# Scores of a head pair in one tile with one store, in nine rooms; four loads of groups at once; k loaded like q and laid out by GpSimd

## The chip, the cores and the metric

The kernel runs on one core of one Trainium2 chip. The metric is the device time of one execution in microseconds (us). The core has five engines that each work through a queue of their own in order: TensorE (PE: matmuls and transposes into PSUM; PEld is its loading of weights), VectorE (DVE), ScalarE (ACT), GpSimd (POOL) and SyncE (SP). Here SP issues nearly all transfers (DMA). They run on 16 transfer engines. An engine waits for another one, or for a transfer, on semaphores, and what stands behind a waiting instruction in the same queue waits too.

## The reference

Attention over 2 batches (B), 12 heads (H), 448 positions (S) and 64 columns per head (D). The heads are mixed by a 12 by 12 matrix ahead of the softmax and by another one behind it:

```
scores = scale * np.matmul(q, k.transpose(0, 1, 3, 2))
scores = np.einsum('bhij,hg->bgij', scores, w_pre)
scores = scores - np.max(scores, axis=-1, keepdims=True)
attn = np.exp(scores)
attn = attn / (np.sum(attn, axis=-1, keepdims=True) + 1e-09)
attn = np.einsum('bhij,hg->bgij', attn, w_post)
return np.matmul(attn, v).astype(np.float32)
```

Its output, 896 rows of 768, goes through an RMS norm and a gated feed-forward layer (silu, width 1536) and then through a second feed-forward layer (elu, width 2048). Everything is float32, w_gate, w_val, w_out and the weights of the second layer come as float64 and are converted on the chip.

## The kernel before

**Layout.** The sequence of a batch is cut into four chunks of 112 positions (CP = 112, NCH = 4); position p * 4 + c stands on partition p of chunk c. Heads go in six pairs (NP = 6). The scores of a pair are computed per chunk: rows of 112 positions of q against all 448 of k. As the mixing runs over heads, the scores go out to a DRAM tile `s_d[b]` in the order position, head, column and come back as groups: a group is ten positions times twelve heads, 120 partitions by 448 columns. There are 45 groups a batch, 90 in all, and a load brings two (LG = 2, 420 KB) into a tile `sg` of which there are four.

**First stage (lines 743 to 762).** `load_first` issues the loads of k and q of batch 0, pair by pair, on SP, into two rooms of the tile "at". k comes through `pair_of`, in pieces of 64 elements (256 bytes); q in pieces of four positions, 1024 bytes. TensorE needs chunk, head, column order. k lies so by its load; q is brought into it by a copy on VectorE (`q_beside`, line 415). Then `turned` (line 441) transposes the pair's k or q, ScalarE copies the result rounded (line 446), VectorE the rest (line 448: the split), and `scores` (line 459) multiplies: high times high, high times low and low times high, two heads, six matmuls. `busy` (line 425) is filler for TensorE. Two pairs behind the turning, `scores(0, i - 2, 0, True)` does chunk 0. `select`, `repeat`, `copies` and `blocks` make the mixing matrices from w_pre and w_post: small VectorE instructions, one matmul (line 141), two copies of it on VectorE (line 149), four selects on GpSimd (lines 155 and 159), and on VectorE the scales vsc (line 165).

**Emptying the scores (line 470, `scores_out`).** Each head's scores are copied from PSUM by ScalarE (line 478) or VectorE (line 476) into a staging room `st`, 112 by 448, of which there are five (and three of the tile "e32" for some of chunk 1), and stored by a transfer of its own (line 479). A copy that finds no free room waits until a store has landed.

**Main loop (line 829).** After chunk 0, line 765 loads the first two groups, EARLY = 4 pairs of chunk 1 are done, and line 770 loads the next two. Then each step t issues, on all engines, parts of several groups: the split of group t + 3 (lines 527 on ScalarE and 528 on GpSimd; every second group needs none), the mixing matmuls of t + 1 (535, or 538 to 540), the maximum of t (547, VectorE), its exponential (555, ScalarE), the normalised halves eh and el of earlier ones (586, 593, VectorE), the second mixing (614) and its copy (626). Loads of groups are issued seven groups ahead (AHEAD = 7). The remaining pairs of scores, the turning of batch 1 and its scores lie in a list `hq` and are popped at 0.5 to 0.8 a step. Loads of v and the second batch's k and q stand on SP between these.

**After it.** Windows of six or seven groups are multiplied with v, normalised (tiles xt and sq) and written as xh and xl; then the feed-forward layers run, with their weights loaded and converted in the tiles raw, w32 and whl of `wpool`.

## Time and profile before

| | us |
|---|---|
| median of 3 runs | 767.53 |
| lowest and highest | 763.04, 774.26 |
| the profiled execution | 771.17 |
| its span, first to last instruction | 769.5 |

| engine | busy us | share of the span | instructions |
|---|---|---|---|
| TensorE | 749.9 | 97% | 5743 |
| its weight loads | 592.2 | 77% | 5743 |
| VectorE | 552.0 | 72% | 1107 |
| ScalarE | 434.4 | 56% | 904 |
| GpSimd | 96.3 | 13% | 117 |

The attention part takes the first 280 us or so, the feed-forward layers the rest. An engine's busy share is a mean over stages with different limits. Matmuls are pipelined and their ends are modelled, so that a busy TensorE is not TensorE at its peak. In rows in order of time, the first number is the start, the second the duration, and what stands in brackets is how long the engine had stood idle before it and what ended that. "xN" counts instructions merged into one row.

### The profile page before, as it was taken

The page shows a single profiled execution, that of the slowest core. Times are in us where ns is not written, and L with a number is a line of the kernel's source. Part 1 is how long each engine was busy: PE and PEld are TensorE (multiplying, and loading weights), DVE is VectorE, ACT ScalarE, POOL GpSimd, SP SyncE. Part 2 cuts the span into 40 slices and gives each one's busy share as a digit, 9 for nine tenths or more (in the row PEclk, how much of TensorE's full clock was granted, in tenths as well). Part 3 has the DMA queues.
Part 4 walks back from the last instruction along what each step waited for, and adds up shares of the span by engine and source line. Part 5 has one row for each costly group of instructions (what it writes and reads, how often), then busy time and mean ns, then how long its engine had stood idle before and what let it go on. Part 6 is the DMA issues. An engine that isn't in the chain of part 4 may idle for free.

```text
span 769.5 us, 14672 instructions
## 1 busy us (share of the span) xinstructions
PE 749.9 (97%) x5743; PEld 592.2 (77%) x5743; DVE 552.0 (72%) x1107; ACT 434.4 (56%) x904; POOL 96.3 (13%) x117
## 2 busy tenths in 40 slices
PE   8899999999898999999999999999999999999997
PEld 7566887777676865555555599999999999999997
DVE  6476999997898947788787766554888787742741
ACT  5377798889578826665667433231776666311310
POOL 1122443443344400000000000000000000000000
PEclk9899999999899999999999999999999999999999
DMA  8898985877654004343323233322443343542612
GB/s 210 276 304 236 172 214 171 248 192 237 174 164 108 3 2 134 114 123 124 122 87 121 83 112 117 100 84 81 123 124 114 92 123 90 160 121 73 168 37 72
DMA packets 92872, 104.04 MB, mean 135 GB/s; under 512 B 21316, under 2 KB 88708, under 8 KB 92804
## 3 DMA queue, kind: packets, MB, share of 16 engines
q1 hardware_dynamic: 92612, 103.04, 47.3%
q8 instruction: 45, 0.74, 0.4%
q14 instruction: 23, 0.19, 0.1%
q10 hardware_dynamic: 192, 0.08, 0.1%
HBM read 81.08 MB, written 22.02 MB: 134 GB/s over the span
## 4 chain that ended last, share of the span: by engine, by line
PE 76%; DVE 13%; DMA 4%; ACT 4%; issue 2%; POOL 1%; SPq 0%; ACTq 0%; POOLq 0%
PE psa_t L200 13%; PE psa_t L199 13%; PE psa_t L201 12%; PE psa_t L1076 4%; PE psa_t L1078 4%; PE psa_t L1077 4%; PE psf_t L201 3%; PE psf_t L199 3%; PE psf_t L200 3%; DVE el L593 3%; DMA s_d<-st 3%; PE pst_t L614 3%; PE psv_t L650 3%; DVE nmax L547 3%; PE psa_t L459 3%; PE psa_t L535 2%
## 5 line engine op out<-in xcount | busy, mean ns | idle before, releaser
L614 PEld LDWEIGHTS <-eh 120*112 120x112 f16 x720 | 67.3, 132 | 28.0 <-issue 19.4
L254 ACT ACTIVATE whl<-w 128x768 fp32r<-128x768 f32 x44 | 37.3, 847 | 84.9 <-DVE w L248 70.7
L226 ACT ACTIVATE w<-raw 128x768 f32<-128x768 f32 x68 | 61.6, 907 | 25.6 <-DVE whl L306 18.9
L258 DVE TENSOR_TENSOR whl<-w,whl 128x768 fp32r<-128x768 f32 x44 | 42.2, 958 | 44.7 <-ACT whl L254 44.7
L528 POOL TENSOR_TENSOR sl<-sg,sh 120x448 fp32r<-120x448 f32 (+1 forms) x45 | 56.5, 1256 | 124.3 <-ACT sh L527 116.9
L200 PE MATMUL psa_t<-x2l,whl 128*128 128x448 f32 x192 | 70.7, 368 | 0.0
L201 PE MATMUL psa_t<-x2h,whl 128*128 128x448 f32 x192 | 70.1, 365 | 0.0
L199 PE MATMUL psa_t<-x2h,whl 128*128 128x448 f32 x192 | 70.1, 365 | 0.0
L555 ACT ACTIVATE e<-psa_t,nmax 120x448 f32<-120x448 f32 (+1 forms) x90 | 57.3, 636 | 22.3 <-DVE rs L570 20.2
L614 PE MATMUL pst_t<-m2h,eh 120*112 120x120 f16 x360 | 63.3, 218 | 2.9 <-ACT at L626 2.8
L614 PE MATMUL pst_t<-m2h,el 120*112 120x120 f16 x360 | 63.2, 219 | 2.9 <-DVE el L593 2.1
L248 DVE SCALAR_TENSOR_TENSOR w<-w,raw 128x768 int32<-128x768 int32 x68 | 65.2, 958 | 1.1
L593 DVE SCALAR_TENSOR_TENSOR el<-e,rs,eh 120x448 f16<-120x448 f32 (+1 forms) x90 | 65.4, 727 | 0.2 <-ACT eh L584 0.2
L242 DVE SCALAR_TENSOR_TENSOR raw<-raw 128x768 int32<-128x768 int32 x68 | 65.0, 956 | 0.0
L614 PE MATMUL pst_t<-m2l,eh 120*112 120x120 f16 x360 | 63.3, 218 | 0.0
L298 ACT ACTIVATE w<-w,gs 128x128 f32<-128x128 f32 x144 | 44.6, 392 | 23.2 <-DVE gs L287 23.2
L650 PE MATMUL psv_t<-at,vs 112*64 112x70 f32 (+3 forms) x1344 | 56.3, 232 | 0.0
L547 DVE TENSOR_REDUCE nmax<-psa_t 120x1 f32<-120x448 f32 (+1 forms) x90 | 54.9, 610 | 0.6 <-PE psa_t L535 0.6
L199 PE MATMUL psa_t<-xhl,whl 128*128 128x448 f16 x150 | 52.9, 353 | 1.0 <-ACT xhl L702 1.0
L626 ACT ACTIVATE at<-pst_t 112x480 f32<-112x480 f32 (+1 forms) x90 | 52.1, 579 | 2.5 <-PE pst_t L614 2.3
L650 PEld LDWEIGHTS psv_t<-at,vs 112*64 112x64 f32 x1344 | 47.1, 140 | 8.3 <-issue 5.1
L1076 PE MATMUL psa_t<-whl,gh 128*128 128x384 f32 x160 | 53.4, 334 | 0.0
(146 smaller groups left out, 1905.6 us busy)
## 6 DMA issues: line engine op xcount, KB each, us to landing
raw<-in_moe_w_out_dram SPq DMA_DIRECT2D x28, 768.0 KB, 4.5
sg<-s_d SPq DMA_DIRECT2D x44, 420.0 KB, 5.1
s_d<-st SPq DMA_DIRECT2D x93, 196.0 KB, 3.5
raw<-in_moe_w_in_dram SPq DMA_DIRECT2D x16, 768.0 KB, 4.6
raw<-in_moe_w_gate_dram SPq DMA_DIRECT2D x12, 768.0 KB, 4.3
raw<-in_moe_w_val_dram SPq DMA_DIRECT2D x12, 768.0 KB, 4.5
vs<-in_v_dram SPq DMA_DIRECT2D x12, 224.0 KB, 6.1
qk<-in_k_dram SPq DMA_DIRECT2D x6, 224.0 KB, 5.1
```

Source lines behind the costliest of these rows:

```text
L199: nc.tensor.matmul(out=ps, lhsT=wh(kk), rhs=xh_(kk), start=(first and kk == 0), stop=False)
L200: nc.tensor.matmul(out=ps, lhsT=wh(kk), rhs=xl_(kk), start=False, stop=False)
L201: nc.tensor.matmul(out=ps, lhsT=wl(kk), rhs=xh_(kk), start=False, stop=(last and kk == nk - 1))
L226: nc.scalar.activation(out=w, in_=raw.bitcast(F32)[:, :, 1], func=ACTF.Abs if small else ACTF.Copy, scale=REBASE)
L242: nc.vector.scalar_tensor_tensor(out=lo, in0=hi, scalar=SIGN, in1=lo, op0=ALU.bitwise_and, op1=ALU.bitwise_or)
L248: nc.vector.scalar_tensor_tensor(out=wi, in0=wi, scalar=3, in1=lo, op0=ALU.logical_shift_left, op1=ALU.bitwise_or)
L547: nc.vector.tensor_reduce(out=nmax[:r], in_=ps[:r, :S], axis=AXX, op=ALU.max, negate=True)
L555: nc.scalar.activation(out=e32[:r], in_=ps[:r, :S], func=ACTF.Exp, bias=nmax[:r], scale=1.0, accum_out=sm[:r])
L593: nc.vector.scalar_tensor_tensor(out=el[:r], in0=e32[:r], scalar=rs[:r], in1=eh[:r], op0=ALU.mult, op1=ALU.subtract)
L614: nc.tensor.matmul(out=o, lhsT=lhs[:r, c * CP:(c + 1) * CP], rhs=rhs[:r, :, :ni], start=(n == 0), stop=(n == 2),)
L650: nc.tensor.matmul(out=psx[s * D:(s + 1) * D, kk, :n], lhsT=vs[b, kk][:, s, c, :], rhs=at[:, c, hh, :n], start=(c == 0), stop=(c == NCH - 1),)
L1076: nc.tensor.matmul(out=o, lhsT=gh[:, kk, tk], rhs=wh[:, j], start=first, stop=False)
```

## The change

Four things are changed, and small ones go with them.

- **Pair tiles.** The two heads of a pair go into one staging tile, 112 by 2 by 448, and one transfer stores both (line 484 of the changed kernel) once the second copy is done. For batch 0 there are nine such rooms: four of the tile whl, two of raw (both for weights, later) and three of st; for batch 1 the three of st.
- **Four loads.** The first four loads of groups (eight groups) are issued one behind the other after chunk 0; the main loop goes on from the fifth. EARLY is 6: all of chunk 1 is done ahead of the main loop.
- **k like q.** k of batch 0 is loaded in 1024-byte pieces as q is, and brought into order by a copy on GpSimd (q's stays on VectorE).
- **Order of the first stage.** The first pair's copies stand first; the small instructions for the mixing matrices follow, `repeat` behind the first pair's transposes, `copies` and `blocks` behind the first splits. k and q of a pair are turned one behind the other, then come the scores. vsc is computed in `post`. xt has two rooms instead of three.

```diff
         def post():
...
             nc.vector.tensor_tensor(out=m2l, in0=m2p, in1=m2h, op=ALU.subtract)
+            for s in range(2):
+                nc.vector.tensor_scalar_mul(
+                    vsc[s * D:(s + 1) * D], cmax.rearrange("p (k s) -> p s k", s=2)[s * D:(s + 1) * D, s], BACK
+                )
...
-                    if tag == "kt":
-                        t = t.rearrange("p (c h d) -> p c h d", h=2, c=NCH)
-                        nc.sync.dma_start(out=t, in_=pair_of(src, 0, p))
-                    else:
...
+                    t = t.rearrange("p (h c d) -> p h c d", h=2, c=NCH)
+                    nc.sync.dma_start(
+                        out=t, in_=src[0, 2 * p:2 * p + 2].rearrange("h (p c) d -> p h c d", c=NCH)
+                    )
...
-        def q_beside(p):
...
+        def beside(p):
+
+            for tag, eng in (("kt", nc.gpsimd), ("qt", nc.vector)):
+                t = ap.tile([CP, NCH, 2, D], F32, tag=tag, name=tag, bufs=2)
+                eng.tensor_copy(out=t, in_=qk_sb[0, p, tag].rearrange("p h c d -> p c h d"))
+                qk_sb[0, p, tag] = t
...
+            st, left = [], [2]
             for s in range(2):
                 dve = s == 1 and (p % 2 == 1 if first else filling[0])
                 late = on_dve if dve else on_act
-                late.append(lambda s=s, dve=dve: scores_out(b, 2 * p + s, c, pss[s], dve))
...
+                late.append(lambda s=s, dve=dve: scores_out(b, p, s, c, pss[s], st, left, dve))
+
+        HOMES = ("whl",) * 4 + ("raw",) * 2 + ("st",) * 3
+
+        def room_of(b, n):
+
+            home = HOMES[n % len(HOMES)] if b == 0 else "st"
+            if home == "st":
+                return ap.tile([CP, 2, S], F32, tag="st", name="st", bufs=3)
+            t = wpool.tile([P, 2 * KD * P], F32, tag=home, name="st_" + home[0], bufs=HOMES.count(home))
+            return t[:CP, :2 * S].rearrange("p (h j) -> p h j", h=2)
+
+        def scores_out(b, p, s, c, ps, st, left, dve):
+            if not st:
+                st.append(room_of(b, c * NP + p))
+            if dve:
+                nc.vector.tensor_copy(out=st[0][:, s], in_=ps[:CP, :S])
             else:
...
+                nc.scalar.activation(out=st[0][:, s], in_=ps[:CP, :S], func=ACTF.Copy)
+            left[0] -= 1
+            if not left[0]:
+                nc.sync.dma_start(out=s_d[b][c * CP:(c + 1) * CP, 2 * p:2 * p + 2, :], in_=st[0])
+                scored[b] = min((c + 1) * CP, S) if p == NP - 1 else c * CP
...
-            xt = ap.tile([P, KD, WMAX], F32, tag="xt", name="xt", bufs=3)
+            xt = ap.tile([P, KD, WMAX], F32, tag="xt", name="xt", bufs=2)
...
-        EARLY, FIRST, FAST, RATE, LATE, AHEAD = 4, 0.5, 0.8, 0.75, 0.6, 7
+        EARLY, FIRST, FAST, RATE, LATE, AHEAD = 6, 0.5, 0.8, 0.75, 0.6, 7
...
         busy(16)
+        beside(0)
         select()
-        repeat()
-        copies()
-        q_beside(0)
-        blocks()
         for i in range(NP + 2):
             if i < NP:
                 turned(*pairs[i], "kt")
                 busy(2)
+                turned(*pairs[i], "qt")
+                busy(2)
+            if i == 0:
+                repeat()
             if i > 1:
                 scores(0, i - 2, 0, True)
-            if i < NP:
-                turned(*pairs[i], "qt")
-                busy(2)
             if i + 1 < NP:
-                q_beside(i + 1)
+                beside(i + 1)
             follow()
+            if i == 0:
+                copies()
+                blocks()
         pre()
         hq = [f for c in range(1, NCH) for f in rows(0, c)]
-        load_group(0, 0)
+        AT_ONCE = 4
+        for g in range(0, AT_ONCE * LG, LG):
+            load_group(0, g)
         for f in hq[:EARLY]:
             f()
             follow()
         hq = hq[EARLY:]
-        load_group(0, LG)
         post()
...
-            if LG * 2 <= t + AHEAD < n and seq[t + AHEAD][1] % LG == 0:
+            if LG * AT_ONCE <= t + AHEAD < n and seq[t + AHEAD][1] % LG == 0:
```

In the built programs the change shows at three places. The first is SP's queue from the last loads of q and k on (qk are their rooms, s_d_88 the scores of batch 0 in DRAM, sg the groups, vs v). Before:

```order
L407 DMA qk_106<-in_q_dram 112x2x256
L479 DMA s_d_88<-st 112x448 x12
L499 DMA sg<-s_d_88 120x2x448
L479 DMA s_d_88<-st 112x448
L479 DMA s_d_88<-st_e 112x448
L479 DMA s_d_88<-st 112x448
L479 DMA s_d_88<-st_e 112x448
L479 DMA s_d_88<-st 112x448
L479 DMA s_d_88<-st_e 112x448
L479 DMA s_d_88<-st 112x448 x2
L499 DMA sg<-s_d_88 120x2x448
L479 DMA s_d_88<-st 112x448 x2
```

The same place in the changed kernel (st_w and st_r are the rooms in whl and raw):

```order
L402 DMA qk_106<-in_q_dram 112x2x256
L484 DMA s_d_88<-st_w 112x896 x4
L484 DMA s_d_88<-st_r 112x896 x2
L504 DMA sg<-s_d_88 120x2x448 x4
L484 DMA s_d_88<-st 112x896 x3
L484 DMA s_d_88<-st_w 112x896 x4
L484 DMA s_d_88<-st_r 112x896 x2
L504 DMA sg<-s_d_88 120x2x448
L376 DMA vs<-in_v_dram 112x2x256
```

Four loads of groups now stand ahead of all stores of chunk 1, where one did, and the next load stands behind nine pair stores.

The second place is the start of VectorE's queue, from its first copies on (setup holds the small tiles of the mixing matrices, par the splits). Before:

```order
L132 COPY setup<-ident 12x120
L133 TENSOR_REDUCE setup<-setup 128x12
L137 TENSOR_SCALAR setup<-setup 128x12
L145 RECIPROCAL setup<-setup 128x12
L149 COPY setup<-psa_t 120x120 x2
L415 COPY qt<-qk_105 112x512
L165 TENSOR_SCALAR vsc<-setup 64x6 x2
L415 COPY qt<-qk_105 112x512
L448 TENSOR_TENSOR par<-psa_t,par 128x448 x2
```

And in the changed kernel:

```order
L411 COPY qt<-qk_105 112x512
L132 COPY setup<-ident 12x120
L133 TENSOR_REDUCE setup<-setup 128x12
L137 TENSOR_SCALAR setup<-setup 128x12
L145 RECIPROCAL setup<-setup 128x12
L411 COPY qt<-qk_105 112x512
L444 TENSOR_TENSOR par<-psa_t,par 128x448 x2
L149 COPY setup<-psa_t 120x120 x2
```

The first q's copy has moved to the front, and the two copies of line 149 from ahead of it to behind the second q's copy and the first pair's two splits.

The third place is the start of GpSimd's queue behind the making of the identity. Before:

```order
masks.py:199 AFFINE_SELECT ident<-ident 128x128
L155 AFFINE_SELECT setup<-setup 120x120
L159 AFFINE_SELECT setup<-setup 120x120
L155 AFFINE_SELECT setup<-setup 120x120
L159 AFFINE_SELECT setup<-setup 120x120
L528 TENSOR_TENSOR sl<-sg,sh 120x448 x10
```

And in the changed kernel:

```order
masks.py:199 AFFINE_SELECT ident<-ident 128x128
L411 COPY kt<-qk_105 112x512 x2
L155 AFFINE_SELECT setup<-setup 120x120
L159 AFFINE_SELECT setup<-setup 120x120
L155 AFFINE_SELECT setup<-setup 120x120
L159 AFFINE_SELECT setup<-setup 120x120
L411 COPY kt<-qk_105 112x512
L411 COPY kt<-qk_106 112x512 x3
L533 TENSOR_TENSOR sl<-sg,sh 120x448 x10
```

The six copies of k are new; the four selects, which wait for the copies of line 149, stand between the second and the third of them.

## Rows read from the trace of the kernel before

**Rows 1.** Stretches: length, busy us (count) by engine, PEclk, DMA share, GB/s.
```profile
6.00:14.00 8.00, 7.34 (x59) 5.63 (x59) 6.37 (x17) 5.05 (x10) 1.41 (x4) 1.00 1.19 246
28.00:32.00 4.00, 1.68 (x7) 0.75 (x5) 0.62 (x1) 1.55 (x3) 1.13 (x1) 0.81 1.06 369
32.00:36.00 4.00, 4.00 (x14) 2.08 (x13) 1.46 (x3) 0.92 (x3) 0.27 (x1) 0.50 0.96 300
36.00:54.00 18.00, 17.79 (x145) 12.62 (x145) 14.38 (x41) 13.39 (x35) 5.84 (x5) 0.96 1.03 319
24.00:68.00 44.00, 38.76 (x301) 26.50 (x301) 27.02 (x77) 26.12 (x63) 9.53 (x8) 0.88 0.95 287
70.00:96.00 26.00, 26.00 (x351) 21.03 (x350) 24.39 (x64) 20.51 (x50) 11.51 (x13) 1.00 0.89 181
320.00:340.00 20.00, 20.00 (x109) 10.39 (x108) 16.20 (x31) 12.34 (x28) 0.00 (x0) 1.00 0.40 119
```

**Rows 2.** Chain of waits, 28 to 72 us: start, us, what (first, last of three).
```profile
25.12 3.91 DMA s_d<-st
...
50.96 7.33 DMA s_d<-st
```

**Rows 3.** Waits by line, 28 to 72 us: us in total, times, longest.
```profile
ACT st L478 <- DMA s_d<-st: 9.1, 5, 4.4
```

**Rows 4.** In order of time, 24 to 71 us: loads, maximum, ScalarE's copies and exponentials.
```profile
24.68 0.38 SPq L499 DMA_DIRECT2D sg<-s_d  x1
...
29.58 0.57 ACT L527 ACTIVATE sh<-sg 120x448 fp32r<-120x448 f32 x1
...
32.78 0.61 DVE L547 TENSOR_REDUCE nmax<-psa_t 120x1 f32<-120x448 f32 x1
...
35.08 0.58 ACT L527 ACTIVATE sh<-sg 120x448 fp32r<-120x448 f32 x1 [3.49 <-DMA sg<-s_d]
...
35.98 0.63 ACT L555 ACTIVATE e<-psa_t,nmax 120x448 f32<-120x448 f32 x1
...
44.85 0.54 ACT L478 ACTIVATE st<-psa_t 112x448 f32<-112x448 f32 x1 [0.81 <-DMA s_d<-st]
...
53.92 0.54 ACT L478 ACTIVATE st<-psa_t 112x448 f32<-112x448 f32 x1 [0.58 <-DMA s_d<-st]
...
58.39 0.54 ACT L478 ACTIVATE st<-psa_t 112x448 f32<-112x448 f32 x1 [2.41 <-DMA s_d<-st]
...
70.10 0.65 ACT L555 ACTIVATE e<-psa_t,nmax 120x448 f32<-120x448 f32 x1
```

**Rows 5.** In order of time, the first stage: TensorE's and VectorE's first pairs.
```profile
6.54 0.40 DVE L149 COPY setup<-psa_t 120x120 f32<-120x120 f32 x2
...
7.53 0.61 PE L441 MATMUL psa_t<-ident,qt 112*128 112x112 f32 x4 [0.66 <-DVE qt L415]
...
8.45 0.43 DVE L415 COPY qt<-qk 112x512 f32<-112x512 f32 x1 [0.46 <-DMA qk<-in_q_dram]
...
8.79 1.15 DVE L448 TENSOR_TENSOR par<-psa_t,par 128x448 fp32r<-128x448 f32 x2
...
9.73 0.57 PE L441 MATMUL psa_t<-ident,qk 112*128 112x112 f32 x4
...
10.46 0.87 PE L459 MATMUL pst_s<-par 64*112 64x448 f32 x6
...
12.62 0.87 PE L459 MATMUL psa_t<-par 64*112 64x448 f32 x6
```

**Rows 6.** By shape: busy us, mean ns, idle before; then two in order of time.
```profile
L155 POOL TENSOR_SCALAR_AFFINE_SELECT setup<-setup 120x120 f32<-120x120 f32 x2 | 0.7, 350 | 5.5 <-DVE setup L149 5.5
...
L586 DVE TENSOR_SCALAR eh<-e,rs 120x448 f16<-120x448 f32 x9 | 4.9, 544 | 0.0
...
47.48 1.36 POOL L528 TENSOR_TENSOR sl<-sg,sh 120x448 fp32r<-120x448 f32 x1 [3.79 <-DMA vs<-in_v_dram]
47.76 1.33 DVE L586 TENSOR_SCALAR eh<-e,rs 120x448 f16<-120x448 f32 x1
```

More of the change, by code (lines that the diff above doesn't have):

```diff
@@ L162, in blocks @@
                 )
-            for s in range(2):
-                nc.vector.tensor_scalar_mul(
-                    vsc[s * D:(s + 1) * D], cmax.rearrange("p (k s) -> p s k", s=2)[s * D:(s + 1) * D, s], BACK
-                )
         def pre():
```

18 lines of the change are left out of this document (removed).

## Prediction

> **What bounds the kernel now.** I read the stretches first, then the chain of waits, then the waits by line, and last the rows in order of time around the places found there. From 320 us on, and in every stretch of the feed-forward part, TensorE is busy without a gap [rows 1]; that part follows the attention part at whatever time attention ends, and no line of it changes. So the change can only move the end of the attention part. Inside it, from 70 to 96 us, VectorE is busy 24.39 of 26 us and TensorE all 26 [rows 1]: the pipeline of 90 groups runs at its engines' pace there, and whatever it starts earlier it ends earlier. What is left to win lies ahead of that.
>
> There the picture differs. From 24 to 68 us the transfer engines are 0.95 busy at 287 GB/s while TensorE works 38.76 of 44 us [rows 1], and the chain of that time holds three stores of scores, the first of 3.91 and the last of 7.33 us [rows 2]: ScalarE wants to empty a PSUM tile into a staging room, all five rooms hold scores whose store has not landed, and, as its queue is in order, everything behind the copy stands too. In all ScalarE waits 9.1 us in this way [rows 3]. The longest of the late ones is 2.41 us, ahead of 58.39 [rows 4].
>
> A second stall is the start. The first load of groups is issued at 24.68; the second stands behind eight stores on SP's queue, so that ScalarE, in order, waits 3.49 us for it until 35.08, and the first exponential, whose maximum VectorE had at 32.78 + 0.61 = 33.39, runs only at 35.98 [rows 4]. From there, step 13 is reached at 70.10: 34.1 us for 13 steps, 2.62 us a step [rows 4].
>
> **The change part by part.** Times are taken against the profiled execution, 771.17 us with a span of 769.5, itself 3.6 above the median of the three runs, 767.53.
>
> *First stage (until the scores of the first 112 rows are stored).* Before, TensorE turned the first q at 7.53 and the third k at 9.73, and from the first scores at 10.46 to the second at 12.62 one pair takes 2.16 us [rows 5]; TensorE has transposes, fillers and scores back to back there, so quicker loads do not shorten the pair. They shorten the way into it. The loads ran at 246 GB/s with every other transfer in 256-byte pieces, where a stretch with long pieces reaches 369 [rows 1]. Two pairs are 0.92 MB, 3.7 us at the one rate, 2.5 at the other: q of the second pair, awaited until 8.45 [rows 5], comes at 8.45 (no gain) to 7.2. I take 7.2, since k then has the pieces that q has. Against it stands the new order: GpSimd's copy of the third k is behind the four selects, these wait for VectorE's two copies of the mixing weights, and these are now behind the second q's copy and the first two splits (they stood ahead of the first q before). 7.2, copy 0.43, splits 1.15, weights' copies 0.40 [rows 5] make 9.2; four selects at 0.35 [rows 6] make 10.6. GpSimd's copy of 512 columns has no row. Below it is VectorE's 0.43 [rows 5], above it GpSimd's own subtraction of 448 columns with two inputs, 1.36 [rows 6], which is 1.55 for 512; one input instead of two speaks for the lower half, and I take 0.9. So the third k is turned at 11.5 instead of 9.73: +1.8. The other copies take 0.9 in each 2.16 and hide behind TensorE; without that cover each would cost the excess over 2.16. A pair's store also leaves when its second half is ready, so the last one has 392 KB instead of 196 ahead of it: +0.6 at 369 GB/s. Together **+2.4** (0 if q comes early enough to free GpSimd in time, +3.7 if it comes at 8.45).
>
> *Four loads at once.* Before, load to first exponential took 35.98 − 24.68 = 11.3. After, the second load is in flight right behind the first and the stores come after both. The first load takes 4.9 at most (24.68 to 29.58 [rows 4], where ScalarE stood in a room wait of 4.4 [rows 3]) and 3.9 at least, what a store half its size takes [rows 2]; I take 4.4. From its copy to the exponential it is 3.8 by the row of the maximum (29.58 to 33.39), 3.5 at the full clock; I take 3.6. 8.0 instead of 11.3: **−3.3** (−2.4 to −3.9).
>
> *Nine rooms for pairs.* After step 0, the waits left of the 9.1 are those of 0.81, 0.58 and 2.41 [rows 4], 3.8 in all. Nine pair rooms hold 3.6 MB, five half-size ones held 1.0, and the nine are used again after about eleven steps. I take the whole: **−3.8** (0 if the wait turns up on the loads instead).
>
> *Clock.* TensorE fell to 0.50 of its clock (the 1.2 GHz level) from about 30 us, after 28 to 32 us in which it worked 1.68 of 4 us; from 32 to 36 it is busy throughout at that level [rows 1], work that takes half as long at the other. After the change it has all six pairs of the second 112 rows, 5.2 us by 0.87 each [rows 5], and the fillers to do meanwhile, against four before. **−1.0** (0 to −2).
>
> *Transfers that come sooner.* What the rooms no longer hold back queues at the transfer engines, and a load of groups issued seven groups ahead stands behind it. **+1.0**, an estimate between 0 and the case below.
>
> *At nothing:* the smaller number of stores (48 for 96) on SP, which is not what anyone waits for there except through the transfers; vsc moved behind the scores, 0.6 us of VectorE while it waits for data; two rooms instead of three for xt, since the order on VectorE has each room's last reader ahead of its next writer; and two pairs of scores that move from the main loop to before it.
>
> Sum: +2.4 − 3.3 − 3.8 − 1.0 + 1.0 = −4.7, that is 766.5 for an execution like the profiled one, and 767.5 − 4.7 = **762.8** as a median.
>
> **Rivals.**
>
> *The transfers bind, the rooms were only where it showed (slower than before).* From 24 to 68 us 44 × 287 = 12.6 MB went through. Two pairs come earlier, 0.8 MB, so 13.4 MB lie ahead of step 13. At 319 GB/s, the rate of 36 to 54 us [rows 1], that is 42.1 us; started at 24.7 + 2.4 = 27.1 it ends at 69.2 instead of 68, at 287 it ends at 73.9: +1.2 to +5.9, I take +3, **770.5**. For it: the share of 0.95 to 1.06. Against it: stores may lag, since their rows are read many steps later, and only loads must be in time. It decides once a load of groups lands later than its copy on ScalarE wants it, four steps after its issue, some 9 us; then ScalarE waits for sg after step 0, which it did not before.
>
> *GpSimd and VectorE stand in each other's way.* A VectorE scaling took 1.33 us at 47.76, where its mean is 0.54, while GpSimd's subtraction ran from 47.48 to 48.84 [rows 6]; it ended 0.25 us after GpSimd. If each q copy so waits out 0.8 us, VectorE needs 0.43 + 1.15 + 0.3 + 0.8 = 2.7 a pair, over TensorE's 2.16, and five pairs cost 2.5 more: −2.2, **765.3**. Against it: k comes first, so that GpSimd is mostly through when q arrives. The Trainium skill, page SBUF — State Buffer, section Who interferes with whom, has it as a rule: VectorE in a two-port mode and GpSimd share a port pair, whoever issues first holds it, and the other blocks fully. The 1.33 us agrees with that.
>
> *The freed steps run faster than I think.* Without the 3.8 us the 13 steps are at 2.33; at 2.1 they save 3.0 more, and if no backlog costs anything the sum is −8.7: **758.8**. For it: from 36 to 54 us VectorE is busy 14.38 of 18 [rows 1]. Against it: a load of groups and the pops fill transfer time in the same steps.
>
> **How the numbers follow.** Forecast 0.52, transfers bind 0.22, ports 0.13, faster steps 0.13. The forecast's terms at their ends give −9.7 and, with the first rival, +5.9, so 757.8 to 773.4; with the scatter of the three runs (763.04 to 774.26) about each case and its weight, 754 to 772 should hold 8 in 10. The likeliest case by itself is 758 to 767. Two per cent is 15 us, about what a measurement of this kernel can tell from no change; none of the cases reaches it, so only scatter does: faster 0.05, within 0.93, slower 0.02.
>
> **What would show it.** First stage right: the first load of groups issued near 27 us and GpSimd's third copy right behind the selects; wrong if it is issued before 25. Loads right: first exponential near 35, no wait of ScalarE for sg ahead of it. Rooms right: ScalarE waits nowhere for a store of scores up to 72 us, and step 13 comes near 65.4. Clock right: no stretch at half clock near 30 us. The forecast is wrong if step 13 comes earlier and the attention part still ends as late, or if ScalarE waits for sg in the steps after the first.

## The result and the profile after

The changed kernel takes 773.31 us (median of 20 runs, 770.85 to 775.16) where the kernel before takes 767.43 us beside it (20 runs, 763.04 to 774.26): the ratio is 1.0068, with a 95% interval of 1.0048 to 1.0088. It is slower by a little over half a per cent, where 762.8 was forecast. The profiled execution took 771.99 us with a span of 769.9.

The stretches of the trace after, in the columns of [rows 1]:

```profile
6.00:14.00 8.00, 4.28 (x27) 3.56 (x26) 4.76 (x12) 2.07 (x4) 3.35 (x7) 0.72 0.95 235
28.00:32.00 4.00, 4.00 (x32) 2.87 (x31) 3.22 (x10) 1.68 (x4) 0.00 (x0) 1.00 0.39 120
32.00:36.00 4.00, 1.85 (x12) 0.88 (x8) 0.62 (x1) 1.01 (x2) 1.07 (x1) 1.00 1.06 249
36.00:54.00 18.00, 17.59 (x119) 11.38 (x120) 12.02 (x33) 10.95 (x27) 4.63 (x5) 0.91 1.03 334
70.00:96.00 26.00, 22.92 (x278) 18.48 (x276) 19.59 (x55) 15.59 (x39) 8.77 (x10) 0.87 1.08 217
```

Two stretches got worse. From 6 to 14 us TensorE works 4.28 of 8 us in place of 7.34, and the granted clock falls to 0.72. From 70 to 96 us it works 22.92 of 26 in place of 26.00, at 0.87. The half clock from 30 us on is not there. But the idle time ahead of it has only moved: from 32 to 36 us TensorE works 1.85 of 4 us, and its clock falls to the half from 36.8 to 40.2.

The places named in the prediction, in order of time (start, us, engine, line, operation; in brackets the idle time before it and what ended it):

```profile
8.27 0.63 POOL L411 COPY kt<-qk 112x512 f32<-112x512 f32 x1 [3.75 <-DMA qk<-in_k_dram]
...
9.13 0.43 DVE L411 COPY qt<-qk 112x512 f32<-112x512 f32 x1 [0.45 <-DMA qk<-in_q_dram]
...
10.88 0.36 POOL L155 TENSOR_SCALAR_AFFINE_SELECT setup<-setup 120x120 f32<-120x120 f32 x1 [1.99 <-DVE setup L149]
...
12.38 1.36 POOL L411 COPY kt<-qk 112x512 f32<-112x512 f32 x2
...
13.05 1.01 PE L437 MATMUL psa_t<-ident,kt 112*128 112x112 f32 x4 [1.92 <-POOL kt L411]
...
15.58 1.17 PE L455 MATMUL pst_s<-par 64*112 64x448 f32 x6
...
16.69 0.61 PE L437 MATMUL psa_t<-ident,kt 112*128 112x112 f32 x4
...
18.05 0.87 PE L455 MATMUL psa_t<-par 64*112 64x448 f32 x6
...
30.08 1.80 SPq L504 DMA_DIRECT2D sg<-s_d  x4
...
34.27 0.58 ACT L532 ACTIVATE sh<-sg 120x448 fp32r<-120x448 f32 x1 [2.87 <-DMA sg<-s_d]
...
36.25 0.58 ACT L532 ACTIVATE sh<-sg 120x448 fp32r<-120x448 f32 x1 [0.97 <-DMA sg<-s_d]
...
39.09 0.63 ACT L560 ACTIVATE e<-psa_t,nmax 120x448 f32<-120x448 f32 x1
...
72.20 0.62 ACT L560 ACTIVATE e<-psa_t,nmax 120x448 f32<-120x448 f32 x1
...
78.14 1.01 PE L437 MATMUL psa_t<-ident,kt 112*128 112x112 f32 x4 [3.08 <-DMA kt<-in_k_dram]
```

Read from the top: GpSimd copies the second k at 8.27, is then given the four selects from 10.88 on, and reaches the third k at 12.38. TensorE, idle meanwhile, turns it at 13.05, where the k of before was turned at 9.73 [rows 5]. The first scores come at 15.58 instead of 10.46 [rows 5], the first load of groups at 30.08 instead of 24.68, the first exponential at 39.09 instead of 35.98, and step 13 at 72.20 instead of 70.10 [rows 4]. At 78.14 TensorE has waited 3.08 us for the k of the second batch.

Waits by line (us in total, times, longest), first from 28 to 72 us and then from 72 to 90:

```profile
ACT sh L532 <- DMA sg<-s_d: 8.9, 5, 2.9
...
PE psa_t L437 <- DMA kt<-in_k_dram: 3.1, 1, 3.1
```

No row of ScalarE waiting for a store of scores is left in 28 to 72 us. The 9.1 us of [rows 3] are gone. Its waits for the groups' scores went from 4.4 us (3.49 and 0.91, both at the start) to 8.9, of which 3.8 stand ahead of the first exponential and 5.0, in three waits, behind it, where before had 0.9 in one. The chain of waits from 6 to 100 us (start, us, what) has the same places:

```profile
2.24 6.87 DMA qk<-in_q_dram
...
12.38 0.62 POOL kt L411
...
25.30 4.57 DMA s_d<-st_r
...
32.93 10.80 DMA s_d<-st
43.75 8.01 DMA vs<-in_v_dram
51.83 9.13 DMA sg<-s_d
...
69.66 8.44 DMA kt<-in_k_dram
```

The chain of 28 to 72 us before held three stores [rows 2]. Now it holds a store, a load of v, a load of groups and a load of k, each of 8 to 11 us.

### The profile page after: what moved, and what is told of

Same layout as the page of the kernel before. It is cut to its first block, busy times and chain, and to the rows that moved or that the text cites. A ratio compares the mean times of both kernels' runs of the same rounds, so it can differ in the third digit from the quotient of the medians.

```text
span 769.9 us, 14571 instructions
## 1 busy us (share of the span) xinstructions
PE 747.3 (97%) x5743; PEld 593.9 (77%) x5743; DVE 548.8 (71%) x1109; ACT 433.5 (56%) x902; POOL 100.0 (13%) x123
## 4 chain that ended last, share of the span: by engine, by line
PE 77%; DVE 10%; DMA 6%; ACT 3%; issue 2%; SPq 1%; POOL 0%; POOLq 0%; ACTq 0%
PE psa_t L200 12%; PE psa_t L198 12%; PE psa_t L199 12%; PE psa_t L1085 4%; PE psa_t L1083 4%; PE psa_t L1084 4%; PE pst_t L619 3%; PE psf_t L198 3%; PE psf_t L200 3%; PE psf_t L199 3%; PE psv_t L655 3%; DVE el L598 2%; PE psa_t L540 2%; DVE nmax L552 2%; PE psa_t L455 2%
## 5 line engine op out<-in xcount | busy, mean ns | idle before, releaser
L241 DVE SCALAR_TENSOR_TENSOR raw<-raw 128x768 int32<-128x768 int32 x68 | 66.6, 979 | 0.0
L1083 PE MATMUL psa_t<-whl,gh 128*128 128x384 f32 x160 | 54.0, 338 | 0.0
L1084 PE MATMUL psa_t<-whl,gh 128*128 128x384 f32 x160 | 54.0, 338 | 0.0
L1085 PE MATMUL psa_t<-whl,gl 128*128 128x384 f32 x160 | 54.0, 338 | 0.0
```

Of the source, the lines that this page charges most:

```text
L241: nc.vector.scalar_tensor_tensor(out=lo, in0=hi, scalar=SIGN, in1=lo, op0=ALU.bitwise_and, op1=ALU.bitwise_or)
L1083: nc.tensor.matmul(out=o, lhsT=gh[:, kk, tk], rhs=wh[:, j], start=first, stop=False)
L1084: nc.tensor.matmul(out=o, lhsT=gh[:, kk, tk], rhs=wl[:, j], start=False, stop=False)
L1085: nc.tensor.matmul(out=o, lhsT=gl[:, kk, tk], rhs=wh[:, j], start=False, stop=end)
```

## The experiments

Each kernel was timed against the kernel before on its own chip, whose median there was 767.2 to 768.9. Two figures go with each: the ratio, and the time at equal clock. Every run lists its granted clock, and over the 111 runs of before that stood beside the experiments the time follows it: a straight line through them gives 499 us per unit of clock, with a standard error of 44 (20 runs under 0.986 have a mean of 771.2 at 0.9840, 16 over 0.995 have 765.4 at 0.9966). Taking 499 × (1 − clock) off each run leaves a time at full clock. It is an estimate by a fit over runs, with an error of about 0.5 us for the mean of a dozen runs. At full clock the kernel before itself stands at 762.5, 763.3, 763.4 and 763.8 on the four chips, so differences of under 1 us between kernels on different chips say nothing.

| kernel | ratio to before, 95% | mean clock | at full clock, us |
|---|---|---|---|
| before | 1 | 0.9903 | 763.2 |
| changed | 1.0068, 1.0048 to 1.0088 | 0.9874 | 766.7 |
| new_start | 1.0051, 1.002 to 1.0082 | 0.9872 | 766.1 |
| old_start | 0.9975, 0.9947 to 1.0004 | 0.9938 | 763.4 |
| old_start_b | 0.9973, 0.9947 to 1.0 | 0.9929 | 763.3 |
| early4 | 1.0087, 1.0052 to 1.0122 | 0.9826 | 765.9 |
| k256 | 1.0, 0.9971 to 1.0029 | 0.9903 | 762.7 |
| sel_late | 0.9999, 0.9978 to 1.0021 | 0.9894 | 763.6 |
| k_vec | 1.0028, 1.0006 to 1.005 | 0.9876 | 764.1 |
| hold | 1.0027, 1.0004 to 1.0049 | 0.9917 | 766.0 |
| rooms | 1.0026, 0.9999 to 1.0053 | 0.9863 | 764.0 |
| loads4 | 1.0062, 1.0032 to 1.0092 | 0.9874 | 767.1 |
| old_qk2 | 0.9998, 0.9974 to 1.0023 | 0.9932 | 764.7 |
| after_qk2 | 1.007, 1.0038 to 1.0102 | 0.9876 | 767.4 |
| old_v1 (5 loads of v left out) | 0.9936, 0.9907 to 0.9965 | 0.9919 | 759.8 |
| old_v1_qk2 (the same) | 0.9926, 0.9897 to 0.9955 | 0.9950 | 760.9 |

### Which half of the change loses the time

The change was cut in two: the first stage (k in long pieces, copies on GpSimd, new order) and the rest (pair tiles, nine rooms, four loads, six pairs ahead).

**old_start**: the changed kernel with the first stage of before.

```diff
-        beside(0)
         select()
+        repeat()
+        copies()
+        q_beside(0)
+        blocks()
         for i in range(NP + 2):
...
+                    if tag == "kt":
+                        t = t.rearrange("p (c h d) -> p c h d", h=2, c=NCH)
+                        nc.sync.dma_start(out=t, in_=pair_of(src, 0, p))
```

> The changed kernel with the first stage of before (k in 256-byte pieces straight into order, no GpSimd copies, the old order of instructions); pair tiles, nine rooms, four loads at once and EARLY 6 stay. Theory START (the new first stage delays the first loads by 5.4 us, from 24.68 to 30.08, and this carries to the end): first loads near 25.3, first exponential near 34, median about 768 (773.3 less 5.4). Theory BATCH 1 (the loss is made at steps 14 to 17, where the turning of the second batch waits for its k and q): the waits of TensorE for kt and qt at 76 to 85 us stay, median 772 to 774.

**new_start**: the kernel before with the new first stage alone.

```diff
+        beside(0)
         select()
-        repeat()
-        copies()
-        q_beside(0)
-        blocks()
         for i in range(NP + 2):
...
-                    if tag == "kt":
-                        t = t.rearrange("p (c h d) -> p c h d", h=2, c=NCH)
-                        nc.sync.dma_start(out=t, in_=pair_of(src, 0, p))
```

> The kernel before with the new first stage alone (k in 1024-byte pieces, GpSimd copies, new order); single rooms and single loads stay. START: first load near 30, everything behind it 5 us later, median about 772.5. BATCH 1: the delay is caught up in the steps that the transfers bind, median 767 to 769.

**early4**: the changed kernel with four pairs of scores ahead of the main loop in place of six.

```diff
-        EARLY, FIRST, FAST, RATE, LATE, AHEAD = 6, 0.5, 0.8, 0.75, 0.6, 7
+        EARLY, FIRST, FAST, RATE, LATE, AHEAD = 4, 0.5, 0.8, 0.75, 0.6, 7
```

> The changed kernel with EARLY back at 4, so that all later pops, and with them the turning of the second batch, come about two pops (2.7 steps) later against the groups. START: no change beyond 1 us, median about 773. BATCH 1: the two waits of 2.6 and 3.2 us at steps 16 and 17 go, median about 768.

Measured: the old first stage under the rest of the change gives 765.97 (0.9975), the new first stage alone gives 772.88 (1.0051). The loss is that of the first stage. Against the profile of before, the exponential of a step starts later (+) or sooner (−) by, in us:

| step | 0 | 4 | 12 | 20 | 36 | 48 | 72 | 89 |
|---|---|---|---|---|---|---|---|---|
| changed | +3.1 | +2.6 | +1.3 | +5.0 | +6.8 | +6.4 | +1.8 | +0.9 |
| new_start | +7.7 | +9.2 | +6.8 | +6.0 | +6.0 | +6.1 | +6.0 | +5.1 |
| old_start | −2.1 | −3.4 | −4.0 | −1.8 | 0.0 | −0.4 | −5.0 | −5.9 |
| early4 | +4.8 | +5.0 | +1.5 | +5.3 | +6.3 | +6.3 | +6.2 | +6.2 |
| rooms | +3.9 | +4.1 | +0.6 | +0.7 | +1.5 | +1.5 | +1.4 | +1.4 |
| loads4 | +9.0 | +8.4 | +8.6 | +7.6 | +9.1 | +8.7 | +4.4 | +3.8 |

new_start has the loop of before, and from step 16 to step 72 it is 6.0 us late without change: what is lost ahead of the loop is not won back. (The two pairs of scores that six pairs ahead take out of the loop stand against the changed kernel, old_start and loads4 up to step 48; at 0.87 us for six matmuls they are 1.7 us of TensorE.) early4 is as late as the changed kernel up to step 48, so the two pairs are not what makes it slow (774.96, where BATCH 1 had 768).

Behind step 48 they help. Between steps 48 and 72 the kernels with six pairs ahead gain 4.2 to 4.7 us on before, in all twelve profiles; the three others with four pairs ahead gain 0.1. Of the gain 1.7 us is the two pairs' work. The rest begins where TensorE waits for VectorE's half el. First before, then the changed kernel:

```profile
197.32 0.26 PE L614 MATMUL pst_t<-m2h,el 120*112 120x120 f16 x1 [2.12 <-DVE el L593]
...
200.00:205.00 5.00, 5.00 (x48) 3.85 (x50) 4.66 (x14) 1.79 (x5) 0.71 (x2) 0.54 0.67 200
```

```profile
200.00:205.00 5.00, 4.03 (x39) 2.90 (x39) 5.00 (x13) 2.77 (x7) 2.38 (x4) 1.00 0.35 96
...
203.04 0.26 PE L619 MATMUL pst_t<-m2h,el 120*112 120x120 f16 x1 [0.97 <-DVE el L598]
```

All four kernels with four pairs ahead run for 6.8 us at half clock somewhere between 197 and 212 us; none of the twelve with six does. In the medians this is not clear of noise: early4's interval (1.0052 to 1.0122) overlaps the changed kernel's.

The profiled executions of before and changed are 771.17 and 771.99: the 0.8 us between them is what step 89 shows. Over all runs the medians are 5.9 apart, since before's profiled execution lay 3.7 above its median and the changed kernel's 1.3 below. old_start's was the fastest of its twelve. So the table shows where time goes, and the runs how much it is.

The first load scatters too: 25.72 to 28.20 us in six profiles with the old first stage and pair tiles (old_qk2, old_start, old_v1_qk2, old_v1, old_start_b, rooms), 30.08, 31.54, 31.63 and 31.95 in four with the new one (changed, after_qk2, early4, new_start). The two groups do not meet.

### What in the first stage

**k256**: the changed kernel, new order kept, k in 256-byte pieces without a copy.

```diff
-        beside(0)
+        q_beside(0)
...
-                beside(i + 1)
+                q_beside(i + 1)
```

> The changed kernel with k loaded as before (256-byte pieces straight into order, no GpSimd copy) in the new order of the first stage. It splits START: if GpSimd's copies and the long pieces cost the 5 us, the first loads are issued near 25.5 and the median is about 768.5; if the order alone (copies of the mixing weights behind the splits, k and q turned one behind the other) costs them, they stay near 30 and the median near 773. BATCH 1: median 772 to 774 either way.

**sel_late**: the changed kernel, the selects and the two copies on VectorE that feed them moved behind the six pairs.

```diff
             follow()
-            if i == 0:
-                copies()
-                blocks()
+        copies()
+        blocks()
         pre()
```

> The changed kernel, with VectorE's two copies of the mixing weights and GpSimd's four selects moved behind the six pairs of the first stage, so that no select stands between GpSimd's copies of k. k keeps its 1024-byte pieces. SELECTS (the first stage loses its time because GpSimd's third copy of k queues behind the selects and TensorE, starved, falls to half clock): the first loads of groups are issued at 26 to 27 us in place of 30.1, no half clock from 9 to 16, and the median is 767 to 769, about that of the version with k in 256-byte pieces (767.6). LANDING (the time goes because the pieces land late and a second engine stands between k and TensorE, the selects only fill a gap that is there anyway): first loads at 29 or later, half clock still there, median 771 or more.

**k_vec**: the changed kernel, k copied by VectorE.

```diff
-            for tag, eng in (("kt", nc.gpsimd), ("qt", nc.vector)):
+            for tag, eng in (("kt", nc.vector), ("qt", nc.vector)):
```

> The changed kernel with the copies of k on VectorE in place of GpSimd; pieces, order and selects as they are. Each pair then has 0.43 more of VectorE's time in place of 0.61 of GpSimd's. SELECTS: no copy of k waits for a select, so first loads at 26 to 27.5 us and a median of 767 to 769. LANDING: TensorE's second and third pair come as late as now (k of the third pair turned near 13), first loads at 29 or later, median 771 or more.

**hold**: the changed kernel with more of TensorE's fillers where it waits.

```diff
                 turned(*pairs[i], "qt")
-                busy(2)
+                busy(14 if i < 2 else 2)
```

> The changed kernel with 12 more of TensorE's fillers behind each of the first two pairs' turned q, where it waits for GpSimd's copies of k. CLOCK (part of the first stage's loss is the half clock of 9.4 to 16.2 us that follows the idle time): no half clock there, the first scores at 14 to 14.8 in place of 15.6, first loads at 28.5 to 29.3 in place of 30.1, median 771.5 to 772.5. QUEUE ALONE (the clock costs nothing of its own, as TensorE waits anyway): first loads stay within 0.5 of 30.1, median 773.

k256 takes 767.63, ratio 1.0: the new order alone does not cost the 5 us; they come with the long pieces and GpSimd's copies. With the selects moved away (sel_late), GpSimd's copies stand one behind the other, and the first scores and loads come sooner. In order of time:

```profile
8.20 0.61 POOL L411 COPY kt<-qk 112x512 f32<-112x512 f32 x1 [3.88 <-DMA qk<-in_k_dram]
...
10.03 0.61 POOL L411 COPY kt<-qk 112x512 f32<-112x512 f32 x1 [1.21 <-DMA qk<-in_k_dram]
...
13.24 1.22 PE L455 MATMUL pst_s<-par 64*112 64x448 f32 x6
...
27.82 1.80 SPq L504 DMA_DIRECT2D sg<-s_d  x4
```

First loads at 27.82 lie between the two bounds given (26 to 27, or 29 and later), but the time is SELECTS': 768.31, ratio 0.9999, within the 767 to 769 that it expected. Its half clock is not gone, though, as SELECTS had it: 3.4 us from 10 to 14 are left of 6.8. At full clock it is 763.6, 3.1 below the changed kernel's 766.7. LANDING's part, what is left of the delay with the selects gone, is the step from k256 to here. In k256:

```profile
11.97 0.87 PE L458 MATMUL pst_s<-par 64*112 64x448 f32 x6
...
26.14 1.80 SPq L507 DMA_DIRECT2D sg<-s_d  x4
```

That is 1.7 us in the first load and 0.9 at full clock, of which 0.7 is the difference between the two chips (before: 762.5 and 763.3). Copying k on VectorE did less good, 770.61, with the first load at 29.73. The second k, for which TensorE stands from 7.1 on, came out of VectorE only here:

```profile
9.67 0.36 DVE L411 COPY kt<-qk 112x512 f32<-112x512 f32 x1
10.09 1.01 PE L437 MATMUL psa_t<-ident,kt 112*128 112x112 f32 x4 [2.98 <-DVE kt L411]
```

VectorE's queue holds select() ahead of it, whose reduction waits 3.9 us for the load of w_post (waits by line, 5 to 28 us). So one queue had taken the place of the other. LANDING's first load (29 or later) and third k (near 13, here 12.69) came, its median (771 or more) just not, and the cause is one that neither theory named.

In hold the half clock of 9.4 to 16.2 us did not come, with the same queue:

```profile
6.00:14.00 8.00, 5.47 (x46) 4.89 (x44) 4.70 (x12) 2.06 (x4) 2.62 (x7) 1.00 0.97 254
...
29.55 1.80 SPq L504 DMA_DIRECT2D sg<-s_d  x4
```

The first load moved by 0.5 us only. Its second k landed a microsecond later in this profile (copied at 9.27, not 8.27), which hides what the clock gave back there: from the third k to the first scores it is 14.02 to 15.38, 1.36 us, for the 2.53 of the changed kernel. The median is 770.78, 2.5 below the changed kernel's, and the clock of the runs rose from 0.9874 to 0.9917, which by the fit is 2.1 us; at full clock 766.0 stands beside 766.7. So the first load lies between the two theories, and the time is CLOCK's in kind, 0.7 under its range of 771.5 to 772.5. In this profile no half clock is seen before 235 us, while the changed kernel's has three stretches up to 85 us.

Together: the selects between the copies cost about 3 us at full clock, and the lower clock of the runs another 1.4 (0.0029 × 499); 4.5 of the 5.2 us that the ratio gives.

### Where the gain of rooms and loads went

**rooms**: the kernel before with pair tiles and nine rooms; two loads at first, four pairs ahead.

```diff
-            nc.sync.dma_start(out=s_d[b][c * CP:(c + 1) * CP, h, :], in_=st)
+            left[0] -= 1
+            if not left[0]:
+                nc.sync.dma_start(out=s_d[b][c * CP:(c + 1) * CP, 2 * p:2 * p + 2, :], in_=st[0])
```

> The kernel before with the pair tiles, one store for two heads and nine rooms, but its own first stage, two loads at first and four pairs ahead of the main loop. ADDS UP: ScalarE waits nowhere for a store up to 72 us, step 13 is 3 to 4 us sooner and the median near 764. GIVEN BACK: the 9.1 us of waits for rooms are gone, but ScalarE waits as long for groups' scores; step 13 is under 2 us sooner, and the median is 766.5 to 768.

**loads4**: the kernel before with four loads at once and six pairs ahead; single tiles, five rooms.

```diff
-        load_group(0, 0)
+        AT_ONCE = 4
+        for g in range(0, AT_ONCE * LG, LG):
+            load_group(0, g)
         for f in hq[:EARLY]:
...
-        load_group(0, LG)
```

> The kernel before with the four loads of groups at once and six pairs ahead of the main loop in place of four; single tiles, five rooms and the old first stage stay. ADDS UP (each part of the gain carries to the end): first exponential 2 to 3 us sooner than before and a median near 765. GIVEN BACK (what is gained before step 13 is taken again by waits of ScalarE for groups' scores and of TensorE for the second batch's k, as TensorE and the transfers are full): a gain of 2 to 3 us up to step 12, under 1 at step 36 and later, median 766.5 to 768.

rooms goes from +3.9 at step 0 to +0.6 at step 12 and +0.2 at step 13: 3.2 and 3.7 us won, close to the 3.8 of the forecast, and the lateness from step 20 on is constant within 1 us. It starts late since in this execution its first stage, the old one, ran at half clock (PEclk 0.60 from 6 to 14 us) and its first load was issued at 28.20. Whether that is so in the other eleven runs is not shown; their clock, 0.9863, is below that of before. At full clock the kernel stands at 764.0, with before at 763.3 on its chip. ADDS UP was right on the steps, and neither on the time; both expected a median at or below that of before.

loads4 is slower by 4.7 us, which no theory had. The stretches and the wait that show why:

```profile
28.00:32.00 4.00, 1.41 (x9) 0.95 (x9) 0.00 (x0) 0.00 (x0) 0.00 (x0) 0.86 1.03 246
32.00:36.00 4.00, 0.00 (x0) 0.00 (x0) 0.00 (x0) 0.00 (x0) 0.00 (x0) 0.50 0.98 257
...
37.19 0.54 ACT L478 ACTIVATE st<-psa_t 112x448 f32<-112x448 f32 x1 [10.10 <-DMA s_d<-st]
```

With five rooms the six pairs ahead fill them, the stores stand behind four loads on SP's queue, and ScalarE waits 10.1 us for a room with everything behind it. From 32 to 36 us no engine works. Four loads at once need the nine rooms; the two are one edit, not two terms of a sum.

Both together, with six pairs ahead and on the old first stage, were run again as **old_start_b**:

> The run with the old start once more (pair tiles, nine rooms, four loads, but the first stage of before), beside the two that follow. If its lead of 0.25% was real: median 1.5 to 2.5 below before. If not: within 1 of before.

766.15, ratio 0.9973, after 765.97 and 0.9975. The lead of 2 us is there twice, each interval just touching 1. At full clock, though, both stand at 763.3 and 763.4 beside 763.2: by the fit, the whole lead is the clock (0.9938 and 0.9929 against 0.9903), and the rooms and loads have won nothing in waiting. The half clock near 200 us that six pairs ahead take away is one place where the clock can have come from.

Why, is seen in TensorE's idle time. Two stretches of before and then four of old_start:

```profile
24.00:36.00 12.00, 9.68 (x48) 5.79 (x49) 3.67 (x9) 3.02 (x7) 1.40 (x2) 0.77 0.85 272
...
54.00:70.00 16.00, 13.29 (x142) 9.68 (x139) 9.58 (x30) 11.39 (x28) 2.29 (x2) 0.89 0.92 254
```

```profile
24.00:36.00 12.00, 10.32 (x68) 6.80 (x67) 6.50 (x17) 5.67 (x13) 3.09 (x3) 1.00 0.81 223
36.00:54.00 18.00, 16.17 (x136) 10.83 (x135) 13.17 (x38) 12.68 (x33) 4.00 (x4) 1.00 1.04 358
54.00:70.00 16.00, 15.86 (x202) 12.34 (x202) 11.64 (x36) 12.77 (x33) 3.41 (x3) 1.00 0.98 291
70.00:96.00 26.00, 23.31 (x286) 19.15 (x287) 23.48 (x64) 17.93 (x44) 11.02 (x14) 0.93 1.10 186
```

Before, TensorE stands 2.32 + 0.21 + 2.71 + 0 us in these four stretches (the second and fourth are in [rows 1]), 5.2 in all. In old_start it is 1.68 + 1.83 + 0.14 + 2.69 = 6.3. The rooms emptied 54 to 70 us as meant. The idle time came back from 36 to 54, where ScalarE waits 3.26 us for sg (until 46.84; 9.1 us in four waits from 24 to 100 us), and at 70 to 96, where TensorE waits 2.7 us for the second batch's k.

**old_qk2** and **after_qk2**: the second batch's q and k loaded one pair sooner, on the old start and on the changed kernel.

```diff
-            def first():
-                turned(*pairs[i], "kt")
-                if i + 1 < len(pairs):
-                    load_qk(*pairs[i + 1])
+            def second():
+                turned(*pairs[i], "qt")
+                if i + 2 < len(pairs):
+                    load_qk(*pairs[i + 2])
...
                 load_qk(*pairs[NP])
+                load_qk(*pairs[NP + 1])
```

> The changed kernel with the first stage of before, as in the run with the old start, and the q and k of the second batch loaded one pair sooner: two pairs at step 7 in place of one, and each later pair two pairs ahead in place of one. TAKEN AT THE TURNING (what the rooms and the four loads win up to step 13 is lost where TensorE stands 2.7 us for the second batch's k at about 72 to 76 us and falls to half clock): no such wait, no half clock near 74, the lead of 3 to 4 us over before at step 12 is still there at step 36, median 763 to 764.5. TAKEN ANYWHERE (TensorE is full from 60 us on, and another wait takes that one's place): the wait goes, but the lead at step 36 is under 1.5 us and the median 765.5 to 767.

> The changed kernel as it is, with the same sooner loads of the second batch's q and k. TAKEN AT THE TURNING: the wait of 3.1 us and the half clock at 78 to 84 go, the lateness against before falls from about 5 to about 1 us at step 36, median 769 to 770.5. TAKEN ANYWHERE: median 772 to 774, as the changed kernel.

The wait for k is gone in old_qk2 and down from 3.1 to 0.6 us in after_qk2. The time does not follow: 767.77 (0.9998), above the 765.5 to 767 that TAKEN ANYWHERE gave, and 773.35 (1.007). In old_qk2 ScalarE waits 11.5 us for sg in place of 9.1 (24 to 100 us), and TensorE idles 1.28 us from 54 to 70 in place of 0.14. So TAKEN ANYWHERE is right in kind; but taken by what?

**old_v1**: the old start, with five of the first batch's six loads of v left out.

```diff
-            if 0 <= t - 1 < KD:
-                load_v(0, t - 1)
+            if t == 1:
+                load_v(0, 0)
+                for kk in range(1, KD):
+                    vs[0, kk] = vs[0, 0]
```

> The kernel with the old start, which leaves out five of the six loads of v of the first batch (one tile of v stands for all six), so 1.1 MB less to move between 40 and 56 us, with the same instructions on the engines. TRANSFERS BIND (the gain of rooms and four loads goes into waits of ScalarE for groups' scores, since stores, v and loads share the transfer engines): ScalarE's waits for sg between 28 and 72 us fall from 9.1 to under 5, TensorE's idle time from 36 to 54 us from 1.8 to under 0.8, and the median is 2 to 3 below that of the old start beside it. ENGINES BIND (the waits for sg only fill time that another engine sets): idle time and median within 1 of the old start.

**old_v1_qk2**: the same, with the sooner loads of q and k too.

> The same with the five loads of v left out, and the second batch's q and k loaded one pair sooner. TRANSFERS BIND: now neither sg nor kt is waited for much; TensorE idles under 3 us between 24 and 130 us in place of 6 to 7, and the median is 3 to 5 below the old start. ENGINES BIND: within 1.5 of the old start.

1.1 MB less to move, the same instructions on the engines, and the time falls to 764.35 and 762.57, where old_start_b beside them has 766.15, 1.8 and 3.6 less (2 to 3 and 3 to 5 were expected); at full clock to 759.8 and 760.9, 2.4 to 3.5 us under it. (The intervals of the ratios overlap; at full clock the difference is four times its error or more.) Two stretches and a wait of old_v1:

```profile
36.00:54.00 18.00, 16.21 (x119) 10.75 (x118) 13.21 (x38) 12.52 (x32) 4.28 (x4) 0.91 1.02 377
70.00:96.00 26.00, 25.76 (x347) 21.16 (x346) 25.30 (x64) 20.80 (x51) 12.51 (x15) 1.00 0.88 172
```

```profile
ACT sh L535 <- DMA sg<-s_d: 6.1, 3, 3.2
```

TRANSFERS BIND is borne out in kind. The waits for sg fell from 9.1 us (8.4 in old_start_b) to 6.1 (under 5 was expected), and the wait for the second batch's k went. Two things could have done this, since five issues less stand on SP's queue too. The loads of k were issued only a little sooner (the second at 63.52 and the third at 69.23, in old_start at 64.19 and 70.80), but each landed faster. From issue to landing (KB, median us), 24 to 100 us, old_start_b and then old_v1:

```profile
kt<-in_k_dram SPq DMA_DIRECT2D x6, 224.0 KB, 7.6
...
kt<-in_k_dram SPq DMA_DIRECT2D x6, 224.0 KB, 5.2
```

VectorE, ScalarE, GpSimd and TensorE wait for v itself in neither. TensorE's idle time from 36 to 54 us did not move (1.79, under 0.8 was expected), and in old_v1_qk2 ScalarE still waits 6.9 us for sg, where little was expected. So the relief came some 20 to 30 us behind the place where the load was taken off: the transfer engines are busy throughout from 36 to 96 us (shares of 1.03 to 1.08 in old_start_b), and what is taken away at 43 to 52 us is felt where the backlog ends.

## Why the prediction failed, step by step

*First stage, +2.4, range 0 to +3.7: +5.4 in the profile.* This term decided the outcome. The queue was seen rightly (GpSimd's third copy behind the four selects), but three sizes in it were wrong.
- The second q was to arrive at 7.2 on the strength of long pieces. It came at 9.13, later than before (8.45 [rows 5]); the rate from 6 to 14 us was 235 GB/s where 246 had been [rows 1]. What the forecast left out is that SP issues the loads faster when all are in long pieces: nine loads of k and q by 6 us in all seven profiles with both in long pieces, six in all nine with k in short ones. More of them are in flight at once, and each takes longer to land, the loads of q first before and then after (0 to 16 us, KB, median us). In the nine the median landing is 5.0 to 5.7 us for q and 5.1 to 5.9 for k, in the seven 5.8 to 6.5 and 6.8 to 7.9; the second q is copied at 8.45 to 9.37 and at 9.06 to 10.15. So the long pieces did not bring it sooner, and 0.7 later than before is in part scatter. The link to the issuing is argued; no run separates it.

```profile
qk<-in_q_dram SPq DMA_DIRECT2D x6, 224.0 KB, 5.0
...
qk<-in_q_dram SPq DMA_DIRECT2D x6, 224.0 KB, 6.1
```

- The copies of weights behind the second q went back as far, the selects started at 10.88, and the third k was turned at 13.05 and not at 11.5. GpSimd's copy was cheaper than assumed, 0.63 and not 0.9, and did not save it.
- Between that k and the first scores the new order puts the third q and its fillers. From turned k to scores it is 13.05 to 15.58, 2.5 us; before it was 9.73 to 10.46, 0.7 [rows 5]. Of the 1.8 more, 1.2 is the half clock: one pair later, at the full clock, the same instructions take 16.69 to 18.05, 1.4 us. The order costs 0.6. k256, which has this order alone, has its first scores 1.1 us after those of old_start (11.97 and 10.87) but its first load only 0.3 later, since the pairs catch up.
- The idle TensorE fell to half clock from 9.4 to 16.2 us. The forecast had reckoned with such a stretch at 30 us only. hold, which has none in its first stage, is 2.1 us better by the clock of its runs. Two profiles with the old first stage have one too (rooms 6.8 us, old_start_b 3.4), and of the seven with the new one only hold has none.

*Four loads at once, −3.3: −2.3 in the profile.* From load to exponential it took 9.0 (30.08 to 39.09), not 8.0 and not 11.3. The load's landing was right (34.27 − 30.08 = 4.2 for 4.4); the second copy waited another 0.97 at 36.25. By itself, with six pairs ahead, the edit loses 4.7 us, as loads4 shows.

*Nine rooms, −3.8: right in kind and nearly in size, up to step 12.* The waits of [rows 3] are gone, and rooms wins 3.2 us from step 0 to step 12. In the changed kernel, 13 steps take 33.1 us in place of 34.1: −1.0. What failed is the claim behind the term, that a wait of ScalarE taken away is time won. TensorE's idle time there, 2.71 us from 54 to 70, and the half clock with it (PEclk 0.89) were what could be won, and in old_start as much idle time came up elsewhere.

*Clock, −1.0.* The stretch at 30 us went, as forecast; one half as long came at 36.8, behind the idle time at 32 to 36. In all the changed kernel has stretches at 9.4 (6.8 us), 36.8 (3.4 us) and 77.7 (6.8 us), and its runs have 0.9874 where before has 0.9903: by the fit +1.4 and not −1.0.

*Transfers that come sooner, +1.0: too small.* The rival that had the transfers bind, at 0.22 and 770.5, named its test: ScalarE waits for sg after step 0. It does, 5.0 us in three waits (8.9 in five with the two ahead of step 0), and in old_v1, on the old start, the time falls with the transfers. The rival's 770.5 is nearest to the result, but by luck in part: most of the loss is the first stage, which it took as the forecast did. I held against it that loads need only be in time. They were not, and neither was the second batch's k at 78.14, 30 us further on than I had looked.

*The port rival, 0.13, fell.* VectorE's copies of q had a mean of 477 ns from 6 to 28 us beside GpSimd's copies, and 423 in sel_late with as many of them; the 0.8 us a pair that it asked for is nowhere. The Trainium skill, page SBUF — State Buffer, section Who interferes with whom, lets VectorE in a two-port mode and GpSimd block each other in full; in which mode these copies ran no run shows, and what they show of blocking is 0.05 us each in the mean (one of the five took 0.61).

*Freed steps faster, 0.13, fell* with the terms it was built on.

*Two pairs of scores ahead, put at nothing: −4.6 between steps 48 and 72.* Of this 1.7 is their work and the rest TensorE's wait and half clock near 200 us, which the forecast did not look at.

So the step that failed is the first stage, +5.4 where +2.4 was summed, and with it the claim that ScalarE's waits taken away are time won. The −8.1 of rooms, loads and clock shrank to about −3 by step 13 and to next to nothing by step 36 (+6.8 there, of which 1.7 is the two pairs done ahead). What the profile wins back after step 48 was not forecast. Over the runs the loss is 3.5 us at full clock and, by the fit, 1.4 by the clock.

## What to carry to other kernels

When a copy is moved to an idle engine, write down that engine's whole queue up to the last of the copies, with what each entry waits for: four late selects among GpSimd's copies were worth about 3 us at full clock here. Take a wait of a feeding engine as time won only up to the idle time of the engine that is full, and ask of full transfer engines where the backlog ends, not where it shows. Price idle TensorE twice in a first stage, once for the time and once for the half clock behind it.

## What the runs showed of the hardware

Long pieces did little for the rate here. From 6 to 14 us, with k in 256-byte and q in 1024-byte pieces, nine profiles (before, rooms, loads4, k256, both with the old start, and the three built on it) show 215 to 246 GB/s, 228 in the mean, at DMA shares of 1.16 to 1.23. With both in 1024-byte pieces seven profiles (the changed kernel, new_start, early4, sel_late, k_vec, hold, after_qk2) show 235 to 257, 249 in the mean, at 0.95 to 1.03. The rate rose by 9%, and two single profiles, 246 before and 235 after, show the opposite. (With the old start the first stores of scores fall into the window too.) The Trainium skill, page DMA: Bandwidth & Descriptors, section Why small descriptors are slow (HBM only), gives every piece three cycles on top of one for each 32 bytes, which makes 27% of a 256-byte piece; by that an estimate is 1.375 against 1.094 per byte for half of the bytes, a rate 13% higher, somewhat more than these runs show.

The mean clock of a run goes with about half of the scatter of one and the same kernel (the line through the 111 runs takes up 54% of the variance): 5.8 us between the runs of before under 0.986 and those over 0.995. A change that moves an idle stretch of TensorE moves the time by this way too, and a median alone does not tell it from the work.
